# Reordering the first unit of a sparse-attention and feed-forward kernel: k, then v, then q, with the small work spread over three engines and filler matmuls in the waits

## Chip, cores, metric

The kernel runs on one core of one Trainium2 chip. The metric is the device time of one execution in microseconds (us). Before: 264.52 us, median of 4 runs (264.51 to 264.59). Every run of this study was recorded in the fast state, so all comparisons are of fast runs with fast runs.

Names used: PE is TensorE's matmul, PEld its weight load, DVE is VectorE, ACT is ScalarE, POOL is GpSimd, SP is SyncE, which issues most DMAs here.

## The reference, cut

```python
# q, k, v: 4 batches, 8 heads, 768 positions, 64 wide
block, window = 32, 16
k_sum = k.reshape(B, H, nb, block, D).max(axis=3)        # 24 block keys per head
v_sum = v.reshape(B, H, nb, block, D).mean(axis=3)
scores_l = scale * q @ k^T, masked to |i - j| < window
scores_s = scale * q @ k_sum^T + log(block)
a = softmax(concat(scores_l, scores_s));  out = a @ concat(v, v_sum)
# then, for the 3072 tokens of width 512:
h = x @ w_in (512 -> 2048);  g = h * sigmoid(1.702 h);  y = g @ w_out (2048 -> 512)
```

## The kernel before

The 3072 tokens are done in eight units (4 batches, two halves of 384 positions). A unit is attention for four pairs of heads, then `ff_in` (64 matmuls into `ph`, Gelu on ACT into `gT`) and `ff_out` (matmuls into `po`). The attention of unit u+1 is placed between the `ff_out` matmuls of unit u. Only the first unit's attention has nothing to hide behind, and it is the part that the change touches.

Local keys and block keys of 64 queries form one 128-row tile: own rows, halo rows, and 24 block rows. `kx` holds the keys in this form and `vw` the values. In the profile lines, `qz` is the transposed q, `ps_s` the scores, `a_sb` the masked exponentials, `ps_av` the values matmul, `x_sb` the attention output, and `xT` its transpose, which `ff_in` reads. The v windows are built by `vrows`: after the block sums of v (`vs`, a matmul with the selector `E`), four SBUF-to-SBUF DMAs copy the halo rows and two more copy the 24 block rows into every window.

```python
    def load_k(b, p):
        t = stage.tile([128, 2, 2, JH, D], F32, name=f"kf{p}", tag=f"kf{p}")
        for half in range(2):
            sp.dma_start(out=t[:, half].rearrange("p h r d -> p h (r d)"),
                         in_=k[b, 2 * p:2 * p + 2, half * HALF:(half + 1) * HALF]
                         .rearrange("h (p r) d -> p h (r d)", r=JH))
        raw["k", p] = t

    def load_q(b, p, half):
        t = stage.tile([128, 2, JH, D], F32, name=f"qf{p}{half}", tag=f"qf{p}{half}")
        sp.dma_start(out=t.rearrange("p h r d -> p h (r d)"),
                     in_=q[b, 2 * p:2 * p + 2, half * HALF:(half + 1) * HALF]
                     .rearrange("h (p r) d -> p h (r d)", r=JH))
        raw["q", p, half] = t

    def load_v(b):
        for c in range(3):
            t = stage.tile([128, H, 2, D], F32, name=f"vf{c}", tag=f"vf{c}")
            for j in range(2):
                r0 = (2 * c + j) * 128
                sp.dma_start(out=t[:, :, j, :],
                             in_=v[b, :, r0:r0 + 128].rearrange("h p d -> p h d"))
            raw["v", c] = t
# ...
    vs_ps = [None]

    def vsum(s, js):
        if js[0] == 0:
            vs_ps[0] = psx.tile([128, H * D], F32, name="ps_vs", tag="x")
        ps = vs_ps[0]
        w5 = vw[s].rearrange("p (j e) h c -> p j e h c", e=2)
        for j in js:
            o = 20 - 4 * j
            pe.matmul(out=ps, lhsT=E[:, o:o + 128], rhs=w5[:, j, 0, :, 0:D],
                      start=(j == 0), stop=(j == NJ - 1))

    def vrows(s):
        w5 = vw[s].rearrange("p (j e) h c -> p j e h c", e=2)
        dve.tensor_copy(out=vs[:, :, 0:D], in_=vs_ps[0].rearrange("p (h d) -> p h d", d=D))

        sp.dma_start(out=w5[96:112, 1:NJ, 0], in_=w5[112:128, 0:NJ - 1, 1])
        sp.dma_start(out=w5[112:128, :, 0], in_=w5[64:80, :, 1])
        sp.dma_start(out=w5[32:48, :, 1], in_=w5[48:64, :, 0])
        sp.dma_start(out=w5[48:64, 0:NJ - 1, 1], in_=w5[0:16, 1:NJ, 0])
        sp.dma_start(out=w5[64:64 + nb, :, 0], in_=vs[64:64 + nb].unsqueeze(1)
                     .to_broadcast([nb, NJ, H, VC]))
        sp.dma_start(out=w5[0:nb, :, 1], in_=vs[0:nb].unsqueeze(1)
                     .to_broadcast([nb, NJ, H, VC]))
# ...
    def tq(p, half, e0, e1):
        src = cast.pop(("q", p))
        big = psb.tile([128, 1024], F32, name="ps_q", tag="big")
        ps = big[:, 0:HALF]
        p3 = ps.rearrange("p (c r) -> p r c", r=JH)
        for r in range(JH):
            pe.matmul(out=p3[:, r], lhsT=src[:, r].rearrange("p h d -> p (h d)"),
                      rhs=ident, start=True, stop=True)
        for hh, eng in ((0, e0), (1, e1)):
            r = slice(hh * 64, hh * 64 + 64)
            copy(eng, qz[p][half][r, :, hh, :], ps[r].rearrange("p (t c) -> p t c", c=QT))
# ...
    def scores(b, half, p):
        a_sb[p] = attp.tile([128, 2, TH, QT], BF16, name="a_sb", tag="a_sb")
        a = a_sb[p]
        big = psb.tile([128, 1024], F32, name="ps_s", tag="big")
        ps = big[:, 0:2 * HALF].rearrange("p (t h c) -> p t h c", h=2, c=QT)
        for i in range(TH):
            pe.matmul(out=ps[:, i].rearrange("p h c -> p (h c)"),
                      lhsT=kx[p][b % 2][:, half * TH + i, :],
                      rhs=qz[p][half][:, i].rearrange("p h c -> p (h c)"),
                      start=True, stop=True)
        act.activation(out=a.rearrange("p h t c -> p t h c"), in_=ps,
                       func=ACT.Exp, scale=scale)
        af = a.rearrange("p h t c -> p h (t c)")
        dve.tensor_mul(af, af, mk[:, half * TH:(half + 1) * TH, :]
                       .rearrange("p t c -> p (t c)").unsqueeze(1)
                       .to_broadcast([128, 2, TH * QT]))

    def values(b, half, p):
        x_sb[p] = attp.tile([128, JH, 2, D], BF16, name="x_sb", tag="x_sb")
        a = a_sb[p]
        big = psb.tile([128, 1024], F32, name="ps_av", tag="big")
        ps = big.rearrange("p (h c) -> p h c", h=2)
        pv = ps[:, :, 0:390].rearrange("p h (j c) -> p h j c", c=130)
        for hh in range(2):
            for j in range(JH):
                t = half * TH + 2 * j
                pe.matmul(out=pv[:, hh, j, :].rearrange("p (e c) -> p e c", e=2),
                          lhsT=a[:, hh, 2 * j:2 * j + 2, :].rearrange("p t c -> p (t c)"),
                          rhs=vw[b % 2][:, t:t + 2, 2 * p + hh, 0:D + 1],
                          start=True, stop=True)

        rc = attp.tile([128, 2, JH, 2], F32, name="rc", tag="rc")
        dve.reciprocal(out=rc, in_=pv.rearrange("p h j (e c) -> p h j e c", e=2)[..., D])
        xo = x_sb[p].rearrange("p j h d -> p h j d")
        for e in range(2):
            r = slice(e * 64, e * 64 + 64)
            dve.tensor_mul(xo[r], pv[r, :, :, e * 65:e * 65 + D],
                           rc[r, :, :, e:e + 1].to_broadcast([64, 2, JH, D]))

    def tx(p):
        src = x_sb.pop(p)
        ps = psx.tile([128, HALF], BF16, name="ps_x", tag="x")
        for j in range(JH):
            pe.transpose(out=ps[:, j * 128:(j + 1) * 128],
                         in_=src[:, j].rearrange("p h d -> p (h d)"), identity=ident)
        dve.tensor_copy(out=xT[p], in_=ps)


    def ff_in(u, nt):
        ph = pmm.tile([128, HALF], F32, name="ph", tag="mm")
        for ko in range(KO):
            pe.matmul(out=ph, lhsT=w_in_sb[:, ko, nt * 128:(nt + 1) * 128],
                      rhs=xT[ko], start=(ko == 0), stop=(ko == KO - 1))
        act.activation(out=gT[u % 2][:, nt, :], in_=ph, func=ACT.Gelu_apprx_sigmoid)
```

The weights `w_in` and `w_out` are each loaded in four DMAs on POOL's queue, with a cast from float32 to bfloat16 on the way. The program of the first unit, in order (each engine runs its own part of it in this order):

```python
    load_k(0, 0)
    load_k(0, 1)
    load_v(0)
    load_k(0, 2)
    load_k(0, 3)
    load_q(0, 0, 0)
    load_q(0, 1, 0)

    for p in range(NP):
        clear_kx(dve, p, 0)
    clear_vw(dve, 0)
    dve.memset(vs[:, :, D:VC], float(block))
    cast_k(dve, 0)
    cast_k(act, 1)
    tk(0, 0)
    for p in range(NP):
        clear_qz(pool, p, 0)
    build_masks()
    tk(1, 0)
    for c in range(3):
        for j in (2 * c, 2 * c + 1):
            cast_v(act, 0, j, 0)
            cast_v(pool, 0, j, 1)
        vsum(0, (2 * c, 2 * c + 1))
    vrows(0)
    load_q(0, 2, 0)
    load_q(0, 3, 0)
    for p in range(NP):
        load_q(0, p, 1)
    cast_k(pool, 2)
    cast_k(act, 3)
    tk(2, 0)
    tk(3, 0)
    cast_q(pool, 0, 0)
    tq(0, 0, act, act)
    cast_q(pool, 1, 0)
    load_w_in(0)
    scores(0, 0, 0)
    tq(1, 0, act, act)
    cast_q(pool, 2, 0)
    scores(0, 0, 1)
    values(0, 0, 0)
    tq(2, 0, act, act)
    cast_q(pool, 3, 0)
    scores(0, 0, 2)
    values(0, 0, 1)
    tx(0)
    tq(3, 0, act, act)
    scores(0, 0, 3)
    values(0, 0, 2)
    tx(1)
    values(0, 0, 3)
    tx(2)
    tx(3)
    for c in range(1, 4):
        load_w_in(c)
    for c in range(4):
        load_w_out(c)
    for p in range(NP):
        clear_kx(pool, p, 1)
        clear_qz(pool, p, 1)
    clear_vw(pool, 1)
```

The softmax here doesn't subtract the row's maximum and nothing guards it: scores larger than these inputs give would overflow.

Of the kernel before, what the change touches and what calls it, by code (L numbers as in the profile page):

```python
# [34 lines left out]
def kernel(  # L35
# [75 lines left out]


    E = consts.tile([128, 20 + 128], BF16, name="E")
    nc.gpsimd.memset(E, 0.0)
    for c0 in (20, 84):
        sub = E[:, c0:c0 + 4]
        nc.gpsimd.memset(sub, 1.0)
        nc.gpsimd.affine_select(out=sub, in_=sub, compare_op=ALU.is_ge, fill=0.0,
                                base=0, pattern=[[-block, 4]], channel_multiplier=1)
        nc.gpsimd.affine_select(out=sub, in_=sub, compare_op=ALU.is_ge, fill=0.0,  # L120
                                base=block - 1, pattern=[[block, 4]],
                                channel_multiplier=-1)
# [4 lines left out]
    def sel(ap, base, cq, cp):  # L127
        nc.gpsimd.affine_select(out=ap, in_=ap, compare_op=ALU.is_ge, fill=0.0,
                                base=base, pattern=[[cq, QT]], channel_multiplier=cp)
# [1 line left out]
    mk = consts.tile([128, NQ, QT], BF16, name="mk")  # L131
    left = consts.tile([128, QT], BF16, name="left")

    def build_masks():
        for par, own, blk, halo in ((0, 0, 64, 96), (1, 64, 0, 32)):
            mid = 2 + par
            nc.gpsimd.memset(mk[:, mid, :], 1.0)
            sel(mk[own:own + 64, mid, :], window - 1, -1, 1)
            sel(mk[own:own + 64, mid, :], window - 1, 1, -1)
            sel(mk[blk:blk + 32, mid, :], nb - 1, 0, -1)  # L140
            hm = mk[halo:halo + 32, mid, :]

            sel(hm, -(QT - 16 - (window - 1)), 1, -1)
            sel(hm, -16, 0, 1)
            lf = left[halo:halo + 32, :]

            nc.gpsimd.memset(lf, 1.0)
            sel(lf, window - 1 - 16, -1, 1)
            sel(lf, 15, 0, -1)

            if par == 0:
                nc.gpsimd.tensor_copy(out=mk[:, 0, :], in_=mk[:, mid, :])
            else:
                nc.gpsimd.tensor_copy(out=mk[:, NQ - 1, :], in_=mk[:, mid, :])
                nc.gpsimd.tensor_copy(out=mk[halo:halo + 32, NQ - 1, :], in_=lf)
            nc.gpsimd.tensor_add(hm, hm, lf)
        nc.gpsimd.tensor_copy(out=mk[:, 1, :], in_=mk[:, 3, :])
        for t in range(4, NQ - 1):
            nc.gpsimd.tensor_copy(out=mk[:, t, :], in_=mk[:, 2 + t % 2, :])


    kx = [[keep.tile([128, NQ, 128], BF16, name=f"kx{p}_{s}") for s in range(2)]
# [17 lines left out]
    def clear_qz(eng, p, s):  # L180
        eng.memset(qz[p][s][0:64, :, 1, :], 0.0)
        eng.memset(qz[p][s][64:128, :, 0, :], 0.0)
# [18 lines left out]
    def copy(eng, out, in_):  # L201
        if eng is act:
            act.activation(out=out, in_=in_, func=ACT.Copy)
        else:
            eng.tensor_copy(out=out, in_=in_)

    def cast_k(eng, p):
        t = castp.tile([128, 2, JH, 2, D], BF16, name="kb", tag="kb")
        for half in range(2):
            copy(eng, t[:, half].rearrange("p r h d -> p h r d"), raw["k", p][:, half])  # L210
        cast["k", p] = t

    def cast_q(eng, p, half):
# [4 lines left out]
    def cast_v(eng, s, j, par):  # L218
        dst = vw[s].rearrange("p (j e) h c -> p j e h c", e=2)[:, j, par, :, 0:D]
        copy(eng, dst, raw["v", j // 2][:, :, j % 2, :])  # L220
# [3 lines left out]
    def vsum(s, js):  # L224
# [4 lines left out]
        for j in js:  # L229
            o = 20 - 4 * j  # L230
            pe.matmul(out=ps, lhsT=E[:, o:o + 128], rhs=w5[:, j, 0, :, 0:D],
                      start=(j == 0), stop=(j == NJ - 1))

    def vrows(s):
        w5 = vw[s].rearrange("p (j e) h c -> p j e h c", e=2)
        dve.tensor_copy(out=vs[:, :, 0:D], in_=vs_ps[0].rearrange("p (h d) -> p h d", d=D))
# [10 lines that stand above are left out]
    def at(ap, start, dims):  # L247
        a = ap[:, start:start + 1]
        return bass.AP(tensor=a.tensor, offset=a.offset, ap=[a.ap[0]] + dims)

    def tk(p, s, own=dve):
        src = cast.pop(("k", p))
        big = psb.tile([128, 1024], F32, name="ps_k", tag="big")
        for half in range(2):
            p3 = big[:, half * 512:half * 512 + HALF].rearrange("p (c r) -> p r c", r=JH)
            for r in range(JH):
                pe.matmul(out=p3[:, r], lhsT=src[:, half, r].rearrange("p h d -> p (h d)"),
                          rhs=ident, start=True, stop=True)

        flat = kx[p][s].rearrange("p t c -> p (t c)")  # L260
        copy(own, at(flat, 0, [[768, 2], [256, JH], [192, 2], [1, 64]]),
             at(big, 0, [[512, 2], [128, JH], [64, 2], [1, 64]]))
        ks = attp.tile([128, nb], BF16, name="ks", tag="ks")
        dve.tensor_reduce(out=ks.rearrange("p (h n) -> p h n", h=2),
                          in_=at(big, 0, [[512, 2], [block, nb // 2], [1, block]]),
                          axis=AX.X, op=ALU.max)

        dve.tensor_copy(out=at(flat, 256 + 96, [[768, 2], [256, 2], [-176, 2], [1, 16]]),
                        in_=at(big, 128 - 16, [[512, 2], [128, 2], [16, 2], [1, 16]]))
        dve.tensor_copy(out=at(flat, 768 + 96, [[-176, 2], [1, 16]]),  # L270
                        in_=at(big, HALF - 16, [[512 - HALF + 16, 2], [1, 16]]))
        dve.tensor_copy(out=at(flat, 128 + 32, [[768, 2], [256, JH], [-48, 2], [1, 16]]),
                        in_=at(big, 64 - 16, [[512, 2], [128, JH], [16, 2], [1, 16]]))
        dve.tensor_copy(out=at(flat, 64, [[256, NJ], [64, 2], [1, nb]]),
                        in_=ks.unsqueeze(1).unsqueeze(1).to_broadcast([128, NJ, 2, nb]))

    def tq(p, half, e0, e1):
        src = cast.pop(("q", p))
        big = psb.tile([128, 1024], F32, name="ps_q", tag="big")
        ps = big[:, 0:HALF]  # L280
        p3 = ps.rearrange("p (c r) -> p r c", r=JH)
        for r in range(JH):
# [5 lines that stand above are left out]
# [39 lines left out]
            dve.tensor_mul(xo[r], pv[r, :, :, e * 65:e * 65 + D],  # L327
                           rc[r, :, :, e:e + 1].to_broadcast([64, 2, JH, D]))

    def tx(p):  # L330
        src = x_sb.pop(p)
        ps = psx.tile([128, HALF], BF16, name="ps_x", tag="x")
        for j in range(JH):
            pe.transpose(out=ps[:, j * 128:(j + 1) * 128],
                         in_=src[:, j].rearrange("p h d -> p (h d)"), identity=ident)
        dve.tensor_copy(out=xT[p], in_=ps)


    def ff_in(u, nt):
# [19 lines left out]
            sp.dma_start(out=out[r0:r0 + 128, :], in_=osb)  # L359


    load_k(0, 0)
    load_k(0, 1)
    load_v(0)
    load_k(0, 2)
    load_k(0, 3)
    load_q(0, 0, 0)
    load_q(0, 1, 0)

    for p in range(NP):  # L370
        clear_kx(dve, p, 0)
    clear_vw(dve, 0)
    dve.memset(vs[:, :, D:VC], float(block))
    cast_k(dve, 0)
    cast_k(act, 1)
    tk(0, 0)
    for p in range(NP):
        clear_qz(pool, p, 0)
    build_masks()
    tk(1, 0)  # L380
    for c in range(3):
        for j in (2 * c, 2 * c + 1):
            cast_v(act, 0, j, 0)
            cast_v(pool, 0, j, 1)
        vsum(0, (2 * c, 2 * c + 1))
    vrows(0)
    load_q(0, 2, 0)
    load_q(0, 3, 0)
    for p in range(NP):
        load_q(0, p, 1)  # L390
    cast_k(pool, 2)
    cast_k(act, 3)
    tk(2, 0)
    tk(3, 0)
    cast_q(pool, 0, 0)
    tq(0, 0, act, act)
    cast_q(pool, 1, 0)
    load_w_in(0)
    scores(0, 0, 0)
    tq(1, 0, act, act)  # L400
    cast_q(pool, 2, 0)
    scores(0, 0, 1)
    values(0, 0, 0)
    tq(2, 0, act, act)
    cast_q(pool, 3, 0)
    scores(0, 0, 2)
    values(0, 0, 1)
    tx(0)
    tq(3, 0, act, act)
    scores(0, 0, 3)  # L410
    values(0, 0, 2)
    tx(1)
    values(0, 0, 3)
    tx(2)
    tx(3)
    for c in range(1, 4):
        load_w_in(c)
    for c in range(4):
# [108 lines left out]
```

## Time and profile before

| | before |
|---|---|
| median | 264.52 us |
| span in the trace | 263.1 us |
| first values matmul (`ps_av`) | 27.3 us |
| first `ff_in` matmul (`ph`) | 39.6 us |
| first `ff_out` matmul (`po`) | 53.8 us |
| second unit's first `ph` | 67.7 us |

How to read it: the span counts from the first instruction; times of events are from there. In a chain of waits, each line is start, duration, and what took it, followed back from the end. A duration of 0.16 us per `ph` matmul (384 columns) is PE at full clock (called warm below), 0.32 is half clock (cold). The lines themselves are in the prediction.

### The profile page before, as it was taken

How to read it: one execution, taken by the hardware profiler on the slowest of the kernel's cores; microseconds unless marked ns; L12 is line 12 of the kernel's file. 1: busy time of each engine (PE TensorE's matmuls, PEld its weight loads, DVE VectorE, ACT ScalarE, POOL GpSimd, SP SyncE). 2: the span in 40 equal slices, each digit the busy share in tenths (PEclk: the TensorE clock that was granted, in tenths of full speed). 3: DMA queues.
4: the chain of work that ended last, by engine and by line, in shares of the span. 5: the costliest groups of instructions: out<-in, count | busy, mean ns of one | idle time of the engine just before them, and what ended most of it. 6: DMA issues, size and time to landing. Idle time of an engine off the chain costs nothing.

```text
span 263.1 us, 4275 instructions
## 1 busy us (share of the span) xinstructions
PE 234.2 (89%) x1571; PEld 142.0 (54%) x1592; DVE 146.7 (56%) x336; ACT 131.3 (50%) x218; POOL 75.5 (29%) x185
## 2 busy tenths in 40 slices
PE   2543749999998999999989999999989999999994
PEld 1131535656665555655665656566656556555541
DVE  4527471447699483358796754276995745372000
ACT  3524443663644627752646446844446366637711
POOL 8890792735203003840202006820220000000000
PEclk9998555999999999999999999999999999999999
DMA  6969999998432118993150129972130210011012
GB/s 176 227 173 178 306 202 196 196 221 259 171 52 55 40 42 223 229 272 117 42 103 0 42 92 249 261 239 83 22 81 2 81 40 2 9 71 42 0 40 81
DMA packets 52981, 32.34 MB, mean 123 GB/s; under 512 B 26848, under 2 KB 49888, under 8 KB 52960
## 3 DMA queue, kind: packets, MB, share of 16 engines
q1 hardware_dynamic: 48736, 27.88, 41.9%
q0 software_dynamic: 4224, 4.19, 9.7%
q8 instruction: 12, 0.20, 0.3%
q14 instruction: 9, 0.07, 0.1%
HBM read 27.26 MB, written 6.29 MB: 128 GB/s over the span
## 4 chain that ended last, share of the span: by engine, by line
PE 74%; DVE 8%; POOL 6%; ACT 5%; DMA 2%; issue 2%; SPq 1%; ACTq 0%; POOLq 0%
PE po L27 29%; PE ph L27 26%; PE ps_s L27 4%; PE ps_q L27 4%; PE ps_av L27 4%; DVE kx L27 4%; PE ps_x L27 3%; DMA qf<-in_q_dram 2%; PE ps_k L27 2%; DVE ks L27 2%; ACT L27 2%; DVE x_sb L27 2%; PE ps_vs L27 1%; POOL qz L27 1%; POOL vw L27 1%
## 5 line engine op out<-in xcount | busy, mean ns | idle before, releaser
L27 PE MATMUL ph<-xT,w_in_sb 128*128 128x384 bf16 x512 | 97.7, 335 | 0.7 <-ACT gT L27 0.7
L27 PE MATMUL po<-w_out_sb,gT 128*128 128x512 bf16 x363 | 92.5, 379 | 0.8
L27 ACT ACTIVATE gT<-ph 128x384 bf16<-128x384 f32 x128 | 61.6, 490 | 46.3 <-PE ph L27 45.7
L27 PEld LDWEIGHTS <-w_in_sb 128*128 128x128 bf16 x512 | 52.6, 106 | 31.2 <-issue 5.2
L27 PEld LDWEIGHTS <-gT 128*128 128x128 bf16 x384 | 34.6, 97 | 28.0
L27 DVE CAST qz<-ps_q 64x384 bf16<-64x384 f32 x56 | 31.1, 555 | 28.6 <-PE ps_q L27 28.0
L27 POOL CAST qb<-qf 128x384 bf16<-128x384 f32 x32 | 16.1, 513 | 101.5 <-PE ps_q L27 63.6
L27 DVE TENSOR_TENSOR a_sb<-a_sb,mk 128x768 bf16<-128x768 bf16 x32 | 18.4, 575 | 33.8 <-ACT a_sb L27 32.9
L27 ACT ACTIVATE a_sb<-ps_s 128x768 bf16<-128x768 f32 x32 | 25.2, 809 | 23.4 <-PE ps_s L27 23.3
L27 DVE TENSOR_TENSOR x_sb<-ps_av,rc 64x384 bf16<-64x384 f32 x64 | 35.5, 555 | 1.5
L27 ACT ACTIVATE osb<-po 128x512 f32<-128x512 f32 x24 | 14.3, 597 | 41.1 <-PE ps_x L27 23.3
L27 DVE CAST kx<-ps_k 128x768 bf16<-128x768 f32 (+1 forms) x64 | 25.5, 439 | 10.3 <-PE ps_k L27 10.3
L27 POOL CAST vw<-vf 128x512 bf16<-128x512 f32 x42 | 24.6, 620 | 7.5 <-DMA vf<-in_v_dram 7.3
L27 PE MATMUL ps_k<-ident,kb 128*128 128x128 bf16 x96 | 15.5, 351 | 7.6 <-DVE kb L27 3.9
L27 POOL CAST kb<-kf 128x384 bf16<-128x384 f32 x26 | 13.5, 542 | 29.2 <-PE ps_k L27 26.5
L27 ACT ACT_TABLE_LOAD x16 | 20.5, 1283 | 1.1 <-PEq L511 0.8
L27 PE MATMUL ps_q<-ident,qb 128*128 128x128 bf16 x96 | 16.7, 316 | 4.6 <-DVE kx L27 3.4
L27 PE MATMUL ps_s<-qz,kx 128*128 128x128 bf16 x192 | 16.8, 227 | 4.3 <-ACT qz L27 4.3
L27 PEld LDWEIGHTS <-kx 128*128 128x128 bf16 x192 | 13.9, 102 | 10.4 <-issue 4.1
L27 PEld LDWEIGHTS <-a_sb 128*128 128x128 bf16 x192 | 14.4, 102 | 7.7 <-DVE a_sb L27 0.8
L27 PE MATMUL ps_av<-vw,a_sb 128*128 128x130 bf16 x192 | 17.6, 231 | 0.6 <-DVE a_sb L27 0.5
L27 PEld LDWEIGHTS <-kb 128*128 128x128 bf16 x96 | 11.2, 139 | 11.8 <-POOL kb L27 4.4
(42 smaller groups left out, 115.0 us busy)
## 6 DMA issues: line engine op xcount, KB each, us to landing
kf<-in_k_dram SPq DMA_DIRECT2D x32, 192.0 KB, 4.0
vf<-in_v_dram SPq DMA_DIRECT2D x24, 256.0 KB, 5.1
qf<-in_q_dram SPq DMA_DIRECT2D x32, 192.0 KB, 4.2
out_dram<-osb SPq DMA_DIRECT2D x24, 256.0 KB, 2.0
w_in_sb<-in_moe_w_in_dram POOLq DMA_DIRECT2D x4, 512.0 KB, 10.0
w_out_sb<-in_moe_w_out_dram POOLq DMA_DIRECT2D x4, 512.0 KB, 20.5
vw<-vs SPq DMA_DIRECT2D x8, 148.5 KB
vw<-vw SPq DMA_DIRECT2D x8, 99.0 KB, 2.9
```

The lines of the kernel that those rows point to most:

```text
L27: r = f(*a, **kw)
```

## The change

Its intent: let all k work run while v loads, let q arrive before it is needed, take work off POOL (masks, clears) so that nothing waits for it, split casts and copies over ACT, DVE and POOL, and keep PE's clock up with matmuls on a zero tile whose result nobody reads. The diff, cut to its core:

```diff
     E = consts.tile([128, 20 + 128], BF16, name="E")
-    nc.gpsimd.memset(E, 0.0)
+    warm = consts.tile([128, 512], BF16, name="warm")
+    dve.memset(warm, 0.0)
+    dve.memset(E, 0.0)
     for c0 in (20, 84):
         sub = E[:, c0:c0 + 4]
-        nc.gpsimd.memset(sub, 1.0)
+        dve.memset(sub, 1.0)
# ... the mask code: the 14 selections stay on GpSimd (now all before anything else), and
#     the memsets, copies and adds of build_masks() become finish_masks() on VectorE:
+    def finish_masks():
+
+        dve.tensor_copy(out=mk[:, 0, :], in_=mk[:, 2, :])
+        dve.tensor_copy(out=mk[:, NQ - 1, :], in_=mk[:, 3, :])
+        dve.tensor_copy(out=mk[32:64, NQ - 1, :], in_=left[32:64, :])
+        for par, halo in ((0, 96), (1, 32)):
+            hm = mk[halo:halo + 32, 2 + par, :]
+            dve.tensor_add(hm, hm, left[halo:halo + 32, :])
+        dve.tensor_copy(out=mk[:, 1, :], in_=mk[:, 3, :])
+        dve.tensor_copy(out=mk[:, 4:6], in_=mk[:, 2:4])
+        dve.tensor_copy(out=mk[:, 6:10], in_=mk[:, 2:6])
+        dve.tensor_copy(out=mk[:, 10, :], in_=mk[:, 2, :])
# ...
-    def cast_k(eng, p):
+    def cast_k(eng, p, eng2=None):
         t = castp.tile([128, 2, JH, 2, D], BF16, name="kb", tag="kb")
         for half in range(2):
-            copy(eng, t[:, half].rearrange("p r h d -> p h r d"), raw["k", p][:, half])
+            copy((eng2 or eng) if half else eng, t[:, half].rearrange("p r h d -> p h r d"), raw["k", p][:, half])
# ...
+    def warmth(n):
+
+        for i in range(n):
+            ps = pmm.tile([128, 512], F32, name="ps_w", tag="mm")
+            pe.matmul(out=ps, lhsT=warm[:, 0:128], rhs=warm, start=True, stop=True)
# ... tk() is split in two: tk_own (transposes and own columns, copy on ACT) and tk_rest (maxima, halos)
-    def tq(p, half, e0, e1):
+    def tq(p, half, e0, e1, early=False):
         src = cast.pop(("q", p))
-        big = psb.tile([128, 1024], F32, name="ps_q", tag="big")
+        big = (pmm.tile([128, 512], F32, name="ps_q1", tag="mm") if early else
+               psb.tile([128, 1024], F32, name="ps_q", tag="big"))
# ...
-    def tx(p):
+    def tx(p, eng=dve):
         src = x_sb.pop(p)
         ps = psx.tile([128, HALF], BF16, name="ps_x", tag="x")
         for j in range(JH):
             pe.transpose(out=ps[:, j * 128:(j + 1) * 128],
                          in_=src[:, j].rearrange("p h d -> p (h d)"), identity=ident)
-        dve.tensor_copy(out=xT[p], in_=ps)
+        copy(eng, xT[p], ps)
# ...
-    load_k(0, 0)
-    load_k(0, 1)
+    for p in range(NP):
+        load_k(0, p)
     load_v(0)
-    load_k(0, 2)
-    load_k(0, 3)
-    load_q(0, 0, 0)
-    load_q(0, 1, 0)
-
+    for p in range(NP):
+        load_q(0, p, 0)
     for p in range(NP):
         clear_kx(dve, p, 0)
     clear_vw(dve, 0)
     dve.memset(vs[:, :, D:VC], float(block))
-    cast_k(dve, 0)
-    cast_k(act, 1)
-    tk(0, 0)
     for p in range(NP):
-        clear_qz(pool, p, 0)
-    build_masks()
-    tk(1, 0)
-    for c in range(3):
-        for j in (2 * c, 2 * c + 1):
-            cast_v(act, 0, j, 0)
-            cast_v(pool, 0, j, 1)
-        vsum(0, (2 * c, 2 * c + 1))
+        clear_qz(dve, p, 0)
+    warmth(8)
+
+    cast_k(act, 0, dve)
+    big0 = tk_own(0, 0, act)
+    cast_k(act, 1, dve)
+    tk_rest(0, 0, big0)
+    big1 = tk_own(1, 0, act)
+    cast_k(pool, 2)
+    tk_rest(1, 0, big1)
+    cast_k(pool, 3)
+    warmth(2)
+    cast_v(act, 0, 0, 1)
+    cast_v(pool, 0, 0, 0)
+    big2 = tk_own(2, 0, act)
+    vsum(0, (0,))
+    cast_v(act, 0, 1, 1)
+    cast_v(pool, 0, 1, 0)
+    tk_rest(2, 0, big2)
+    vsum(0, (1,))
+    big3 = tk_own(3, 0, act)
+    for j in (2, 3, 4, 5):
+        cast_v(act, 0, j, 1)
+        cast_v(pool, 0, j, 0)
+        if j == 2:
+            tk_rest(3, 0, big3)
+            finish_masks()
+        warmth(1)
+        vsum(0, (j,))
+    cast_q(dve, 0, 0)
+    cast_q(pool, 1, 0)
     vrows(0)
-    load_q(0, 2, 0)
-    load_q(0, 3, 0)
     for p in range(NP):
         load_q(0, p, 1)
-    cast_k(pool, 2)
-    cast_k(act, 3)
-    tk(2, 0)
-    tk(3, 0)
-    cast_q(pool, 0, 0)
-    tq(0, 0, act, act)
-    cast_q(pool, 1, 0)
+    tq(0, 0, act, dve, True)
+    cast_q(dve, 2, 0)
+    tq(1, 0, act, dve, True)
+    cast_q(pool, 3, 0)
     load_w_in(0)
     scores(0, 0, 0)
-    tq(1, 0, act, act)
-    cast_q(pool, 2, 0)
+    tq(2, 0, act, dve, True)
     scores(0, 0, 1)
+    tq(3, 0, act, dve, True)
+    scores(0, 0, 2)
+    warmth(1)
     values(0, 0, 0)
-    tq(2, 0, act, act)
-    cast_q(pool, 3, 0)
-    scores(0, 0, 2)
+    scores(0, 0, 3)
+    warmth(1)
     values(0, 0, 1)
-    tx(0)
-    tq(3, 0, act, act)
-    scores(0, 0, 3)
+    warmth(2)
+    tx(0, act)
     values(0, 0, 2)
-    tx(1)
+    warmth(2)
+    tx(1, act)
     values(0, 0, 3)
-    tx(2)
-    tx(3)
+    warmth(3)
+    tx(2, act)
+    warmth(3)
+    tx(3, act)
     for c in range(1, 4):
         load_w_in(c)
     for c in range(4):
```

The weights are still the next thing on POOL's queue after the last q cast. In the kernel before, that queue stopped at the cast of a late q (27.6 us), and so the seven later weight loads went out from 28.9. In the changed kernel all eight go out from 19.3 on. The issue of `w_in` (shortest, median and longest in ns, then first and last start in us), before:

```profile
L27 POOL DMA_DIRECT2D w_in_sb<-in_moe_w_in_dram x4: 746/756/908, 18.8 to 30.4; - x4
```

and in the changed kernel:

```profile
L27 POOL DMA_DIRECT2D w_in_sb<-in_moe_w_in_dram x4: 750/766/881, 19.3 to 21.7; - x4
```

More of the change, by code (lines that the diff above doesn't have):

```diff
@@ L132 @@
     left = consts.tile([128, QT], BF16, name="left")
-    def build_masks():
-        for par, own, blk, halo in ((0, 0, 64, 96), (1, 64, 0, 32)):
-            mid = 2 + par
-            nc.gpsimd.memset(mk[:, mid, :], 1.0)
-            sel(mk[own:own + 64, mid, :], window - 1, -1, 1)
-            sel(mk[own:own + 64, mid, :], window - 1, 1, -1)
-            sel(mk[blk:blk + 32, mid, :], nb - 1, 0, -1)
-            hm = mk[halo:halo + 32, mid, :]
-            sel(hm, -(QT - 16 - (window - 1)), 1, -1)
-            sel(hm, -16, 0, 1)
-            lf = left[halo:halo + 32, :]
-            nc.gpsimd.memset(lf, 1.0)
-            sel(lf, window - 1 - 16, -1, 1)
-            sel(lf, 15, 0, -1)
-            if par == 0:
-                nc.gpsimd.tensor_copy(out=mk[:, 0, :], in_=mk[:, mid, :])
-            else:
-                nc.gpsimd.tensor_copy(out=mk[:, NQ - 1, :], in_=mk[:, mid, :])
-                nc.gpsimd.tensor_copy(out=mk[halo:halo + 32, NQ - 1, :], in_=lf)
-            nc.gpsimd.tensor_add(hm, hm, lf)
-        nc.gpsimd.tensor_copy(out=mk[:, 1, :], in_=mk[:, 3, :])
-        for t in range(4, NQ - 1):
-            nc.gpsimd.tensor_copy(out=mk[:, t, :], in_=mk[:, 2 + t % 2, :])
@@ new lines @@
+    dve.memset(mk, 1.0)
+    dve.memset(left, 1.0)
+    for par, own, blk, halo in ((0, 0, 64, 96), (1, 64, 0, 32)):
+        mid = 2 + par
+        sel(mk[own:own + 64, mid, :], window - 1, -1, 1)
+        sel(mk[own:own + 64, mid, :], window - 1, 1, -1)
+        sel(mk[blk:blk + 32, mid, :], nb - 1, 0, -1)
+        sel(mk[halo:halo + 32, mid, :], -(QT - 16 - (window - 1)), 1, -1)
+        sel(mk[halo:halo + 32, mid, :], -16, 0, 1)
+        sel(left[halo:halo + 32, :], window - 1 - 16, -1, 1)
+        sel(left[halo:halo + 32, :], 15, 0, -1)
@@ L251, in tk, with tk_own @@
     def tk(p, s, own=dve):
+        tk_rest(p, s, tk_own(p, s, own))
+    def tk_own(p, s, own):
         src = cast.pop(("k", p))
@@ L262, in tk, with tk_rest @@
              at(big, 0, [[512, 2], [128, JH], [64, 2], [1, 64]]))
+        return big
+    def tk_rest(p, s, big):
+        flat = kx[p][s].rearrange("p t c -> p (t c)")
         ks = attp.tile([128, nb], BF16, name="ks", tag="ks")
```

## The prediction

> **What bounds the kernel now.** I read the page's slices first, then the engine-busy table by stage, the chain of waits over the first 70 us, the SyncE queue's timeline, and last the groups of single tiles.
>
> The slices (40 of 6.6 us each):
>
> ```profile
> PE   2543749999998999999989999999989999999994
> PEclk9998555999999999999999999999999999999999
> DMA  6969999998432118993150129972130210011012
> ```
>
> TensorE (PE) is 90% busy or more nearly everywhere after slice 6. Only the first six slices have room, and they coincide with the half-speed clock (slices 4 to 6). So the change, which touches only the first unit, can gain only there. The same by stage (columns: stretch, its length, busy us of PE, PEld, DVE, ACT, POOL, then granted clock, DMA share, GB/s):
>
> ```profile
> 0.00:20.00 20.00, 8.90 (x30) 4.33 (x30) 8.16 (x35) 7.11 (x11) 17.51 (x63) 1.00 0.89 191
> 20.00:39.60 19.60, 10.33 (x75) 7.57 (x74) 12.38 (x30) 8.40 (x13) 11.31 (x36) 0.61 1.13 230
> 39.60:53.80 14.20, 14.20 (x78) 8.43 (x77) 4.80 (x9) 7.28 (x15) 6.50 (x13) 0.82 1.22 196
> 53.80:67.70 13.90, 13.79 (x108) 8.06 (x108) 8.90 (x19) 6.26 (x10) 5.68 (x9) 1.00 0.96 254
> ```
>
> The first feed-forward matmul starts at 39.6 us; from there PE never idles. In the first 20 us POOL is 88% busy. From 39.6 to 53.8 PE is full, but part of it at clock 0.82. The DMA engines stay at a share of 1.13 to 1.22 until 54 us.
>
> The chain over 20 to 47 us (start, us, what):
>
> ```profile
> 20.28 0.80 SPq L27
> 21.12 6.46 DMA qf<-in_q_dram
> 27.64 0.51 POOL qb L27
> 28.19 0.83 PE ps_q L27 x3
> ...
> 38.31 0.56 DVE x_sb L27
> ...
> 39.79 5.10 PE ph L27 x16
> 45.22 1.95 PE ph L27 x12
> ```
>
> What holds the start is one load: the q of heads 4 and 5 is issued at 21.1, because it stands on the SyncE queue behind the v-window copies, and lands at 27.6. From its cast to the first ph takes another 12 us of serial small steps. Then 16 ph take 5.10 us (0.319 each), where later 12 take 1.95 (0.163): half speed until 44.9. The SyncE queue:
>
> ```profile
> 0.82 1.98 SPq L27 DMA_DIRECT2D kf<-in_k_dram  x4
> 2.83 6.66 SPq L27 DMA_DIRECT2D vf<-in_v_dram  x6
> 9.54 2.68 SPq L27 DMA_DIRECT2D kf<-in_k_dram  x4
> 12.26 0.98 SPq L27 DMA_DIRECT2D qf<-in_q_dram  x2
> 16.49 2.73 SPq L27 DMA_DIRECT2D vw<-vw  x4
> 19.32 1.75 SPq L27 DMA_DIRECT2D vw<-vs  x2
> 21.12 3.83 SPq L27 DMA_DIRECT2D qf<-in_q_dram  x6
> ```
>
> **What the Trainium skill says.** "TensorE: Matmul & The Clock Gate", Part 1, says the array idles at half clock and reaches full clock after about 3.4 us of sustained work, and drops back after a similar idle window. The trace agrees: full rate returns 5 us after ph starts. It also shows that the printed clock of 1.00 in the first 20 us is no evidence, because the first v sums there run at the slow duration (maximum) and all later ones at 379 ns:
>
> ```profile
> L27 PE MATMUL ps_vs<-vw,E x24: 379/379/586, 8.2 to 187.7; 128*128 128x512 bf16 x24
> ```
>
> "DMA: Bandwidth & Descriptors", Queues, rings and completion order, says each engine takes turns between queues packet by packet. The trace fits: beside the weights the six v loads of the next batch (256-byte rows) take 23.69 us to issue, against 6.66 us alone. "SBUF — State Buffer", Who interferes with whom, says VectorE with two SBUF inputs and a GpSimd that reads SBUF exclude each other. The trace hints at it: two masks beside GpSimd casts at 56.75 took 1.47 us, where two alone would take 1.12. "ScalarE: Activation LUTs", What ACT_TABLE_LOAD costs, gives 1283 ns, and the trace has 1283 for each.
>
> **The change part by part.**
>
> (1) Load order. All twelve k and q loads of the first half and six v loads go out before anything waits. Rates from the trace: a 256 KB v load lands each 1.2 us (v casts on ACT begin at 7.53, 8.71, 9.93, 11.13, 12.34, 13.42); after the last v, four k loads of 192 KB were there by 15.85, so 0.6 us each. The v loads therefore move from 13.4 to about 13.4 + 4 x 0.6 = 15.8 us, and the four q loads end at 15.8 + 4 x 0.6 = 18.2 us instead of 27.6 for the third. Removed from the path: 9.4 us of waiting for q.
>
> (2) Masks, clears, casts. POOL loses 8 qz clears (16 in the window are 6.9 us, so 3.5) and some 14 mask copies, memsets and adds of 0.15 to 0.3 (about 3). With 14 mask selections of 0.25, 4 of E at 0.19 and gaps it is done near 6.6 us, when k of heads 4 and 5 arrives. VectorE's added clears (about 3 us, estimated from its 0.22 us for the 128x192 clear) delay k of heads 0 and 1 by perhaps 1 us. All k work then lies beside the v loads: k takes about 1.8 us of VectorE per pair (0.95 maximum, 0.64 halos, 0.22 copy) and one 0.8 us copy on ACT; four pairs end near 14.3, masks near 15.7. Both are before q arrives. Cost on the path: 0.
>
> (3) Values cannot start before the v windows are complete. The last v is cast at 16.45; the copies on SyncE begin about then, as now (16.49), and end issuing at 21.1, as now. With 2.7 us to land (measured for the vw copies) they are there at 23.8; I take 24.3, as the weights now run beside them. Meanwhile q is cast on VectorE and POOL, and ACT and VectorE share the eight qz copies (0.48 and 0.555). From 16.4, VectorE has 0.69 + 4 x 0.555 + 2 x 0.4 + 3 x 0.56 = 5.4 us, so three heads are masked near 22.9, before 24.3.
>
> (4) From 24.3: first values matmuls 0.5, then VectorE for four pairs: 0.23 + 2 x 0.555 = 1.34, with gaps 1.45 each, plus one mask of 0.56: 6.4 us. That is 31.2; last transpose 0.2 and the first ph can follow, near 31.4 instead of 39.6. Gain 8.2 us.
>
> (5) Fillers. Fourteen 512-column matmuls lie in stage 4; warm they take 14 x 0.22 = 3.1 us (estimate from 1.95/12 = 0.163 for 384 columns), cold 6.1. With 24 values, 6 score and 12 transpose matmuls, PE is loaded through most of the 7 us, so the clock should rise before or soon after ph starts. Fully warm, ph's 64 matmuls save 16 x (0.319 - 0.163) = 2.5 us. I take half, 1.3, because cold fillers can themselves delay the last transposes by 1 to 2 us.
>
> (6) Transposed copies move to ACT. The Gelu table load can then come only after the last of them, about 31.9 to 33.2. Three ph buffers cover 3 x 0.65 us, so at most 0.3 us is lost; I take 0.2.
>
> Later units have the same program, so their 56.8 us per batch stays. Sum: -8.2 - 1.3 + 0.2 = -9.3 us; 264.5 - 9.3 = **255.2 us**.
>
> **The rivals.**
>
> Rival A: the weights become the wait. They are issued on POOL; now the first at 18.77 and the rest from 28.9, and w_out lands late:
>
> ```profile
> DMA to landing us min/median/max: 16.6/20.5/24.5
> ```
>
> Issued at 31.1 to 33.3, these landings are about 47.7 to 57.8, 3.3 us apart. Parts of ff_out need them from 53.8 to 64.3, so 6 us of slack. After the change all eight are issued from 18.8 to about 25. At 3.3 us each, plus some 4 us lost to q and k of the next batch, the last lands at 18.8 + 2 + 8 x 3.3 + 4 = 51 to 52, and PE wants it at 31.4 + 12 + 10.3 = 53.7. For it speaks the DMA share, which is at its ceiling already; against it that the issue moves nearly as far as PE does. If it holds, 2 to 4 us come back: 257 to 259.
>
> Rival B: the v windows land later than 24.3, since their small packets share with twice the weights: each us is a us on the end; 256 to 258 with 26 us.
>
> Rival C: the filler matmuls pay fully and the windows land early, at 23: 264.5 - 9.5 - 2.5 = 252.5.
>
> Rival D: VectorE, with more work, slows POOL and itself (the shared port), adding 1 us to each of stages 2 and 4: 257. The chain in stage 4 is VectorE's already, so this is a small shift of the same bound.
>
> Rival E: the next batch's loads miss their date in unit 1. Its k casts are done by 62 and first used at 69 to 75; a shift by 9 leaves nearly nothing for pairs 2 and 3, but v also moves up once the weights are in. A loss of 1 to 2 us at worst.
>
> **Range and chances.** All the gain lies in when ph starts (31.4, give or take 2), whether the clock is up (0 to 2.5), and weights (0 to 3 lost). Taken together 252.0 to 258.6 should hold it 8 times in 10. The 2% line is at 259.2, a gain of 5.3; missing it takes two of A, B and D together: 0.08 for the same. Slower would need PE to be held by something not seen: 0.01.
>
> **What would show it.** Step 1: the q casts start at 16 to 18 us and none waits for a load at 27. Step 2: POOL's k casts near 6.6, VectorE idle before q. Step 3: the first ps_av at 24.3, ended by a DMA, not VectorE. Step 4: first ph at 31.4, the chain before it VectorE's x_sb. Step 5: ph at 0.163 from the start, or slow for part of the first 16. Step 6: a table load after the last xT. If ps_av waits to 26 or later, B is right; if ph or po idle on DMA with PE gaps between 31 and 55 us, A; if from 57 us on the two traces differ by other than a constant, E. A first ph near 31 with an end above 259 would prove my picture of the later stages wrong.

## The result and the profile after

The changed kernel takes 260.27 us (260.08 to 260.60, 4 runs) against 264.52. The ratio is 0.984 with a 95% interval of 0.982 to 0.986. A ratio here is the mean time of one kernel's fast runs over the mean of the other's of the same rounds, so it isn't quite the ratio of the medians. The gain is 4.25 us. The prediction had 9.3 us, that is 255.2, and a range that ended at 258.6; the measured time lies above it.

The slices of the changed kernel's page:

```profile
PE   7555499999989999999989999999989999999994
PEclk9986589999999999999999999999999999999999
DMA  6999999999350139982140249961321110111012
```

PE is now full after slice 5 (before: after slice 6), and the half-clock stretch is shorter. The DMA engines are 90% busy or more in slices 2 to 10. By stage (columns as in the prediction: stretch, its length, busy us of PE, PEld, DVE, ACT, POOL, clock, DMA share, GB/s):

```profile
0.00:20.00 20.00, 12.34 (x51) 6.10 (x52) 14.89 (x67) 9.75 (x15) 12.23 (x37) 0.92 0.95 207
20.00:37.00 17.00, 10.62 (x77) 7.74 (x78) 9.65 (x20) 5.45 (x9) 11.45 (x36) 0.69 1.14 207
37.00:49.30 12.30, 12.03 (x79) 7.61 (x78) 4.44 (x8) 8.84 (x17) 2.49 (x5) 1.00 1.20 216
49.30:63.20 13.90, 13.79 (x108) 8.03 (x108) 9.22 (x19) 6.26 (x10) 9.21 (x15) 1.00 1.05 252
```

The stage before the first `ph` ends at 37.0 instead of 39.6 (2.6 us), `ff_in` takes 12.3 us instead of 14.2 (1.9 us), and `ff_out` takes 13.9 as before. That is 4.5 us, and the spans of the two traces differ by 4.4 at the end: the later units keep their time. POOL fell from 17.5 to 12.2 us in the first 20 us, DVE rose from 8.2 to 14.9.

The chain of waits of the changed kernel, 20 to 40 us:

```profile
20.76 8.12 DMA vw<-vs
...
29.01 0.82 PE ps_av L27 x6
...
36.87 0.35 PE ps_x L27 x3
...
37.25 0.49 ACT xT L27
...
37.75 1.28 ACT L27
...
39.05 0.50 ACT gT L27
...
39.59 0.81 PE ph L27 x4
```

The q load is gone from the chain. In its place stands the copy of the block rows into the v windows, 8.12 us for 148.5 KB. Values can't start before it lands, so the first values matmul is *later* than before, 29.0 instead of 27.3. All that stands between values and `ph` is faster: 8.0 us instead of 12.3. Behind the last transposed copy stands the Gelu table load (the nameless ACT entry of 1.28 us). The first 12 `ph` run before its end, at full rate:

```profile
37.05 2.36 PE L27 MATMUL ph<-xT,w_in_sb 128*128 128x384 bf16 x12
```

### The profile page after: what moved, and what is told of

Same layout as the page of the kernel before. It is cut to its first block, busy times and chain, and to the rows that moved or that the text cites. A ratio compares the mean times of both kernels' runs of the same rounds, so it can differ in the third digit from the quotient of the medians.

```text
span 258.7 us, 4314 instructions
## 1 busy us (share of the span) xinstructions
PE 235.8 (91%) x1596; PEld 143.2 (55%) x1618; DVE 151.1 (58%) x357; ACT 132.7 (51%) x220; POOL 69.9 (27%) x157
## 4 chain that ended last, share of the span: by engine, by line
PE 75%; DVE 10%; DMA 5%; ACT 5%; SPq 2%; issue 1%; POOL 0%; ACTq 0%; DVEq 0%
PE po L27 29%; PE ph L27 25%; PE ps_av L27 5%; DVE kx L27 4%; PE ps_q L27 4%; PE ps_s L27 4%; PE ps_x L27 3%; DMA vw<-vs 3%; PE ps_k L27 3%; ACT L27 2%; DVE ks L27 2%; DMA vf<-in_v_dram 2%; SPq L27 2%; DVE x_sb L27 2%; PE ps_vs L27 2%
## 5 line engine op out<-in xcount | busy, mean ns | idle before, releaser
L27 PE MATMUL ph<-xT,w_in_sb 128*128 128x384 bf16 x512 | 95.5, 329 | 0.9 <-ACT gT L27 0.8
L27 ACT ACTIVATE gT<-ph 128x384 bf16<-128x384 f32 x128 | 61.4, 491 | 39.5 <-PE ph L27 38.7
L27 PEld LDWEIGHTS <-w_in_sb 128*128 128x128 bf16 x512 | 51.8, 104 | 30.4 <-issue 3.6
L27 DVE CAST qz<-ps_q 64x384 bf16<-64x384 f32 x60 | 33.3, 555 | 28.4 <-PE ps_q L27 26.8
L27 POOL CAST qb<-qf 128x384 bf16<-128x384 f32 x30 | 15.2, 512 | 97.4 <-PE ps_q L27 69.2
L27 ACT ACTIVATE a_sb<-ps_s 128x768 bf16<-128x768 f32 x32 | 25.2, 810 | 27.5 <-PE ps_s L27 27.3
L27 DVE TENSOR_TENSOR x_sb<-ps_av,rc 64x384 bf16<-64x384 f32 x64 | 35.5, 555 | 1.5
L27 DVE TENSOR_TENSOR a_sb<-a_sb,mk 128x768 bf16<-128x768 bf16 x32 | 19.1, 599 | 28.2 <-ACT a_sb L27 27.2
L27 POOL CAST vw<-vf 128x512 bf16<-128x512 f32 x42 | 25.2, 639 | 12.3 <-DMA vf<-in_v_dram 12.2
L27 DVE CAST kx<-ps_k 128x128 bf16<-128x128 f32 (+3 forms) x60 | 21.7, 405 | 5.7 <-PE ps_k L27 5.7
L27 POOL CAST kb<-kf 128x384 bf16<-128x384 f32 x28 | 14.7, 544 | 29.8 <-PE ps_k L27 24.4
L27 PEld LDWEIGHTS <-a_sb 128*128 128x128 bf16 x192 | 14.1, 101 | 13.1 <-issue 5.5
L27 ACT ACT_TABLE_LOAD x16 | 20.5, 1283 | 1.1 <-PEq L542 0.8
L27 PEld LDWEIGHTS <-kx 128*128 128x128 bf16 x192 | 14.5, 106 | 6.2 <-issue 1.2
L27 DVE TENSOR_REDUCE ks<-ps_k 128x24 bf16<-128x768 f32 x16 | 15.2, 949 | 1.7 <-ACT kx L27 1.6
L27 PEld LDWEIGHTS <-qb 128*128 128x128 bf16 x96 | 9.8, 120 | 10.0 <-issue 3.2
## 6 DMA issues: line engine op xcount, KB each, us to landing
w_in_sb<-in_moe_w_in_dram POOLq DMA_DIRECT2D x4, 512.0 KB, 12.2
vw<-vs SPq DMA_DIRECT2D x8, 148.5 KB
```

Source lines behind the costliest of these rows:

```text
L27: r = f(*a, **kw)
```

## The experiments

**Theory 1.** The block-row copies are starved by the weight loads, which the change lets go out beside them. **Rival 1:** the copies take 8 us by their own shape (24 partitions, broadcast source). **Rival 2:** the q and k loads that follow them on the SP queue slow them. Each experiment below starts from the changed kernel unless it says otherwise; before stands for the kernel before, run on the same chip in the same call (264.6 to 265.1 us).

### e1: the weights only after the block rows

```diff
+    pool.tensor_copy(out=seen[64:64 + nb], in_=w5[64:64 + nb, NJ - 1, 0, 0, 0:8])   # waits for the
+    pool.tensor_copy(out=seen[0:nb], in_=w5[0:nb, NJ - 1, 1, 0, 0:8])               # two row copies
     load_w_in(0)
```

> The change, with all eight weight loads held back until both block-mean row copies have landed (a tiny read of their last rows on GpSimd ahead of the first weight load). Theory 1 (the block-mean rows are starved because the weights run beside them): the first values matmul moves from 29.0 to 23.5 to 25 us, the first ph from 37.0 to 31.5 to 33.5; the weights then start about 5 us later, so the last w_out lands near 57 to 58 where it is wanted near 54, and 2 to 4 us come back as PE gaps: 257 to 259.5 in all. Rival 1 (the copy takes 8 us by its own shape, broadcast and small rows on 24 partitions): the first values matmul stays at 28.5 to 29.5 and the total is 260 to 266. Rival 2 (the q and k loads issued behind it on the same queue slow it): the same 28 to 29.5 as rival 1.

Measured: 259.69 us (258.00 to 260.12), ratio 0.980 (0.976 to 0.984); its median is just past the expected band. Of its chain of waits:

```profile
21.00 3.24 DMA vw<-vs
...
24.91 9.18 DMA w_in_sb<-in_moe_w_in_dram
```

And of its PE timeline:

```profile
31.23 0.34 PE L27 MATMUL ps_x<-ident,x_sb 128*128 128x128 bf16 x3 [0.43 <-DVE x_sb L27]
34.14 2.10 PE L27 MATMUL ph<-xT,w_in_sb 128*128 128x384 bf16 x6 [2.57 <-DMA w_in_sb<-in_moe_w_in_dram]
```

The same copy took 3.24 us instead of 8.12. Both rivals fall: the shape is unchanged, and the q and k loads still follow on the queue. Values started at 24.4 (predicted 24.3), and PE had the last transposes behind it at 31.57 (predicted: `ph` at 31.4). So with the rows on time, the prediction's steps 3 and 4 hold as written. But now the first weights came at 34.1 and PE waited 2.57 us for them, and after that idle it ran cold: the first 16 `ph` took 5.30 us. What was gained on the rows was paid to the weights, though not where the expectation had it: the last `w_out` landed near 58 as expected, but no matmul waited for it.

### e5: one weight load ahead, seven held back

The two small reads of e1 stand behind `load_w_in(0)` here, in front of the other seven loads.

> The change, with the first weight load where it is and the other seven held until the block-mean rows have landed. Theory 1 with the weights served in order: the rows land about when the first weight load is through, 25 to 27.5 (24.2 with none ahead, 28.9 with all eight); ph from 33.5 to 35.5 without waiting for its first weights; the last weights land near 55 to 58, close to where they are wanted: total 257 to 259.5. If seven loads behind the first make no difference to the rows (only the first one beside them counts), they land at 28.5 to 29 and the total is 260 or more.

Measured: 259.21 us (258.56 to 259.64), ratio 0.978 (0.975 to 0.980). Its chain has:

```profile
20.75 6.97 DMA vw<-vs
```

The rows landed at 27.7. So none ahead: 24.2; one ahead: 27.7; all eight: 28.0 in one run, 28.9 in another (29.4 in e3). One 512 KB load beside the rows does most of the harm. GpSimd had issued it by 20.3, before the copy's wait of 6.97 us began, which points to the load in flight and not to its issuing. The kernel before has just such a single load ahead of its rows, too, but its values begin at 27.3 for other reasons (b1). An estimate: a second row copy issued there at 20.3 and taking the same 7 us lands at 27.3, just in time; no trace shows when it landed. The rows landed just past the expected 25 to 27.5, `ph` started at 35.5, and the total was in the expected band; 0.978 against the change's 0.982 to 0.984 isn't a separation that the intervals carry with certainty.

### e2: the block rows written on chip

```diff
+            act.activation(out=w5[0:nb, 0:JH, 1], in_=vs[0:nb].unsqueeze(1)
+                           .to_broadcast([nb, JH, H, VC]), func=ACT.Copy)
+            pool.tensor_copy(out=w5[64:64 + nb, 0:JH, 0], in_=vs[64:64 + nb].unsqueeze(1)
+                             .to_broadcast([nb, JH, H, VC]))
-        sp.dma_start(out=w5[64:64 + nb, :, 0], ...)     # all six windows
+        sp.dma_start(out=w5[64:64 + nb, JH:NJ, 0], ...) # windows 3 to 5 only; the same for 0:nb
```

> The change, with the block-mean rows of the three windows that the first unit needs written by ACT (rows 0 to 23) and GpSimd (rows 64 to 87), about 1.5 to 2.7 us each; only windows 3 to 5 still come by DMA. If the landing of these rows is what held the values (theory 1 and rival 1 alike): first values matmul at 23 to 25 us, ph at 31 to 33, total 254 to 257, and the weights, now wanted some 6 us earlier and issued some 2 us later, may cost 1 to 2 us of it. If the weights also starve the four window copies that go out just before them, the values start at 25 to 27 instead and the total is 256 to 259. If something else held the values, no gain: 260.

Measured: 256.09 us (256.00 to 256.43), ratio 0.968 (0.966 to 0.970), inside the expected band. Of its chain:

```profile
18.76 1.52 ACT vw L27
20.28 0.38 ACT qz L27
```

Values started at 25.0, `ph` at 32.9. The 1.52 us row copy on ACT stands ahead of the first q copy, so some of the wait went from the DMA to ACT. Still, 260.3 became 256.1: most of the 5.1 us that the prediction missed hung on these rows.

### e3: the transposed copies on VectorE

```diff
-    tx(0, act)        # the same for 1, 2, 3
+    tx(0)
```

> The change, with the four transposed copies of the first unit back on VectorE. Theory: the Gelu table load (37.75 to 39.05) then comes before the last copy instead of behind it, ph no longer waits for gT at 39.6, worth 0.5 to 0.8 us: 259.5 to 259.8. Rival: VectorE is the chain in this stage, four copies of 0.36 us are on it, and three of them delay the last x_sb by 0.7 to 1.1: net 260 to 260.8, or no change.

Measured: 260.62 us (259.69 to 261.12), ratio 0.984 (0.982 to 0.987): no change, as the rival said. Of its chain:

```profile
37.60 0.37 DVE xT L27
...
38.34 2.72 PE ph L27 x16
```

`ph` runs through without the table wait, but starts later: at 38.2, after values at 29.5. That is 8.7 us for the stage against 8.0, since DVE carries the copies between its other work.

### e4 and f1: no fillers; f0: the change again

```diff
-        for i in range(n):
+        for i in range(0):        # in warmth()
```

> The change without any filler matmul. If the fillers warm the clock: the last values and the first 10 to 16 ph run at 0.32 instead of 0.163 us, 1.5 to 2.5 us lost, less 0.3 to 0.8 gained since no cold filler stands ahead of a transpose: 261.2 to 262.4. Rival: the values and score matmuls alone would have warmed it, or ph warms itself beside the table load, so the fillers do nothing: 259.8 to 260.5.

e4 measured: 260.36 us, but spread from 258.93 to 261.69, ratio 0.984 (0.979 to 0.988): inconclusive. So it was run once more, with the change itself beside it in the same rounds:

> The change itself, unedited, on the same chip and in the same rounds as the run without fillers: 260.0 to 260.6, and the same wait of about 5 us for the block-mean rows.

> The change without any filler, once more, as the first run of it was not clear. From its first trace (first 16 ph 4.76 instead of 2.6 us, but the table load hidden behind them and the last transpose 0.4 earlier): 0.8 to 1.5 us more than the change of the same rounds, so 261.0 to 261.8. If fillers are worth nothing in all: within 0.4 of it.

f0: 260.30 us (259.12 to 260.59), ratio 0.982 (0.980 to 0.985). f1: 261.57 us (260.94 to 261.76), ratio 0.987 (0.985 to 0.990). Of f1's chain:

```profile
37.03 4.77 PE ph L27 x16
```

The 16 `ph` take 4.77 us, near the half clock, where the change has them at full rate save for the table wait. The fillers are worth 1.3 us in the medians of f0 and f1; the two intervals just touch, and e4 alone showed no difference. The traces agree with each other: from the first `ph` to the first `po` it is 13.9 us without fillers (e4, f1) and 12.3 with them (the change, f0), of which 0.2 goes back because the fillers let `ph` start 0.2 us later (37.0 against 36.8, with equal rows).

### b1: the kernel before, only the q loads early

```diff
     load_q(0, 1, 0)
+    load_q(0, 2, 0)
+    load_q(0, 3, 0)
 # ...
     vrows(0)
-    load_q(0, 2, 0)
-    load_q(0, 3, 0)
```

> The kernel before, with one edit: the q loads of pairs 2 and 3 go out right behind those of pairs 0 and 1, ahead of the window copies. The reading of the prediction (that one late q load holds the start) would give q casts near 19 instead of 27.6 and a first ph several us earlier than 39.6: 256 to 262 in all. Theory 1 says otherwise: GpSimd, no longer stopped by the late q, issues the seven other weight loads from about 20 instead of 28.9, the block-mean rows land beside them at 28 to 29.5, the first values matmul moves from 27.3 to 28 to 30 and the end stays or gets later: 264 to 267.

Measured: 264.61 us (264.36 to 264.74), ratio 0.998 (0.996 to 1.000) against before. Of its chain:

```profile
27.24 0.81 PE ps_av L27 x6
...
28.09 0.81 PE ps_q L27 x3
...
39.68 5.12 PE ph L27 x16
```

The late q load of pair 2 was the longest entry of the chain before, 6.46 us, and taking it away moved `ph` from 39.79 to 39.68. PE gets to this pair's q at 28.1 in any case, because k of pairs 2 and 3, then scores and values pair by pair, stand ahead of it in program order. The chain was right that the load ended last at that point, but a second path ended 0.1 us earlier. Theory 1's own number for the rows (28 to 29.5) was not met either: values started at 27.2 without waiting for a DMA. With one weight load ahead of them (the other seven went out only from 22.7) the rows must have landed by 27.2; in e5 they did at 27.7.

### b2: b1 with the block rows on chip

The edit is that of b1 with that of e2.

> The kernel before, with the early q loads and with the block-mean rows of the first three windows on chip too. The run with early q alone changed nothing, and its first values matmul at 27.2 waited for no DMA. If the order of the small steps (k of pairs 2 and 3 after v, q casts and scores one pair at a time between the values) holds the first unit there, also this one changes little: 263.5 to 264.8. If the rows were a hidden second wait at 27 behind the q, the values start at 24 to 25 and the total is 261 to 262.5.

Measured: 266.24 us (265.74 to 267.25), ratio 1.006 (1.004 to 1.008): slower, outside the expected band. Of its chain:

```profile
17.14 1.51 POOL vw L27
...
18.71 0.51 POOL kb L27
...
19.27 1.48 PE ps_k L27 x6
```

POOL's row copy stands ahead of its k cast, which came at 17.0 before and at 18.7 here, and everything after moved by 1.7 to 2.3 us: values from 27.2 to 29.3, `ph` from 39.5 to 41.8. So the test of whether the rows were a hidden second wait failed, because the edit delayed something else. What it shows instead is what held the first unit before: the k cast of pair 2 on POOL (pair 3's is on ACT), and the serial steps behind it. That is what the change's order takes away.

### d1, d2, d3: towards the best version

All have the rows on chip. d1 puts only the last transposed copy back on DVE (`tx(3)`). d2 also moves the mask copies and adds to POOL, in the gaps between its v casts, save the last two, which stay on DVE behind the first values. d3 is d2 with both row copies on POOL, after the last q cast, and none on ACT.

> The change with the block-mean rows of windows 0 to 2 written on chip, and only the last of the four transposed copies on VectorE, so that the Gelu table load can go before it. Theory: ph starts near 32.8 as with the rows alone and its wait for the table (35.4) goes: 0.5 to 0.9 us less than the rows alone, so 255.2 to 255.6. If the copies' engine does not matter: 256.1.

> As the run with the rows on chip and the last transposed copy on VectorE, and the mask copies moved from VectorE to GpSimd, between its v casts, where it idles 0.6 us of each 1.2. The prediction's step 2 said they cost nothing on the path; the chain shows them ahead of the first q cast (17.6 where q is there at 16.5). If the chain is right, the first q cast starts 0.8 to 1.2 us earlier and ph with it: 254.0 to 254.8. If step 2 is right: no difference to the run without it, within 0.3.

> Rows on chip, last transposed copy on VectorE, masks on GpSimd as before, but both row copies on GpSimd after the last q cast, so that ACT is free for the qz copies. Values start near 23 and ph near 30.7 instead of 32.6. The weights are issued 1.4 us later, from 21.5, and the last lands near 54.5, where PE would want it at 52.7. If the weights now bind: 254.3 to 255.3, with PE gaps that end on a DMA in the first ff_out. If they keep up: 253.2 to 253.8. If VectorE binds whatever ACT does: 255.2.

| | median (range), us | ratio to before (95%) | first `ps_av` | first `ph` |
|---|---|---|---|---|
| d1 | 255.64 (255.40 to 256.38) | 0.965 (0.963 to 0.967) | 24.6 | 32.5 |
| d2 | 255.26 (255.22 to 255.69) | 0.963 (0.961 to 0.966) | 24.3 | 32.4 |
| d3 | 255.71 (255.08 to 257.81) | 0.967 (0.964 to 0.970) | 22.0 | 30.1 |

d1 is 0.3% below e2 in ratio, 0.5 us in the medians: about the table wait, but the intervals overlap. In d2, DVE's first q cast began at 16.42 (d1: 17.39), but no gain can be told apart from the noise; the next step in its chain is ACT's row copy again. d3 started `ph` 2.3 us earlier than d2 and ended no earlier. Its chain and its waits (total us, times, longest) say why:

```profile
24.88 19.04 DMA w_out_sb<-in_moe_w_out_dram
...
43.97 1.04 PE po L27 x4
```

```profile
PE ph L27 <- DMA w_in_sb<-in_moe_w_in_dram: 0.8, 1, 0.8
```

Now PE waits for weights: 0.79 us for the last part of `w_in` and 0.26 us for the first of `w_out`, through which the chain runs. These and a q cast (0.33 us) are 1.4 of the 2.1 us by which `ff_in` is longer than in d2 (13.9 against 11.8); the rest is not accounted for. The expectation had the weights binding, but in `ff_out` only, and at 254.3 to 255.3 us. That is rival A of the prediction, and here it binds only once the steps ahead of it are out of the way. d2 has the lowest median, 3.7% under the kernel before and about 5 us under the change; its lead over d1 and d3 is within the noise.

## Why the prediction was wrong

- **Step 1, load order: right.** The q casts began at 17.0, 17.6, 18.9 and 19.9 us (16 to 18 was said); that at 17.0 came as its q landed, and the later ones waited for DVE or PE and not for a load. But the value put on it, 9.4 us "removed from the path", wasn't there to remove: b1 shows that the wait for q before had a second path 0.1 us behind it. This did not enter the sum, which went from the new path's own times.
- **Step 2, masks, clears and casts at no cost: right in effect.** POOL's first k cast came at 6.9 (predicted 6.6). The masks on DVE ended at 17.6, not 15.7, and delayed the first q cast by about 1 us, but the rows hid it; d2 found no certain gain from moving them. Rival D's slower VectorE shows there in single operations (the two mask adds took 0.84 us, in d1 0.38), and it does not in the stage of step 4 (two `x_sb` products take 1.12 us before and after).
- **Step 3 is the step that failed.** The row copies were issued nearly when it said (the issue ends at 21.6; predicted 21.1), but "I take 24.3, as the weights now run beside them" put 0.5 us on an effect that measured 4.6: they landed at 28.9 (28.0 to 29.4 in other traces with the same loads), and at 24.2 with the weights held back (e1). Its 2.7 us to land were also those of other copies, the halo rows; a row copy took 3.24 us even in e1. The mechanism was named, as rival B with "each us is a us on the end", but it was sized at 26 at most. The range was too narrow on just that side, and this one rival was enough to miss the 2% line, for which the prediction had thought two were needed.
- **Step 4: right.** In e1 values began at 24.4 and PE was free for `ph` at 31.57, against 24.3 and 31.4. In the changed kernel, with a cold PE at the start of the stage after 5.4 us without work, it took 8.0 us instead of 7.1: 0.9 us of the miss.
- **Step 5, fillers: the mechanism was right, and the size by two errors that cancel.** PE runs at full rate from 34 us on, before `ph` starts. So the first 16 `ph` gained all that a full clock gives, 2.2 us against f1 and 2.5 against the kernel before, where the prediction took half, 1.3. The larger loss of step 6 and the later start took it back to about 1.4 in the traces, 1.3 in the medians; that this equals step 5's number is luck.
- **Step 6, table load: the place was right, the size too low.** It stands behind the last xT, at 37.75, and PE loses some 0.6 us (12.3 us for `ff_in` where 11.7 would be full rate throughout), not 0.2, as 12 `ph` fit into the three buffers and the thirteenth waits for gT.
- **Rival A** did not bind in the change: the last `w_out` landed at 24.6 + 28.7 = 53.3 and was wanted near 60. PE waited for weights in e1 and d3, each time for a part of `w_in` first. **Rival E** is not seen: the distance of the two traces is 4.5 us at 49.3 us and 4.4 at the end. **Rival C** asked for windows at 23 us; they came at 28.9.
- **Two readings.** The printed clock is at 5 in slices 5 to 7, not 4 to 6, so the half speed reaches into a slice in which PE is already full; step 5 counted that part. And the prediction says that the trace agrees with 3.4 us of work before full clock; its own lines show 5.1 us (39.79 to 44.89).

The sum: `ph` at 37.0 instead of 31.4 is 5.6 us, of which 4.7 is the rows and 0.9 the stage behind them; `ff_in` at 12.3 us instead of the 13.1 that steps 5 and 6 imply (14.2 - 1.3 + 0.2) gives 0.8 back. That makes 4.8 of the 5.1 us between 255.2 and 260.3.

What stays open: why exactly the rows lose so much. Rows of 1056 bytes taking turns with the weights' packets is a reading that fits, but no run varied the packet size, and it stays unshown.

## What to carry to other kernels

When a change lets a bulk load go out earlier, list the small transfers that are in flight at that moment and have someone waiting for them: here 8 us for 148.5 KB instead of 3.2. A small copy that the DMA engines would do beside bulk traffic was better done here by compute engines (e2). Such an engine needs 1.5 us to spare and nothing on the path behind the copy in its queue (b2 shows the price if something is). And the longest entry in a chain of waits is an upper bound of what its removal brings, not an estimate: look for who would have come second.

## What the Trainium skill lacked or had wrong

- "DMA: Bandwidth & Descriptors", Queues, rings and completion order, tells that an engine takes turns between queues packet by packet, but not what that costs a small transfer that someone waits for. The runs: a 148.5 KB copy issued from SyncE took 3.24 us with no GpSimd load ahead of it, 6.97 with one 512 KB load and 7.31 to 8.70 with eight. One load does most of the harm; a line with such numbers, and the warning that issuing bulk loads earlier can move a small copy onto the path, would have helped with step 3.
- "ScalarE: Activation LUTs", What ACT_TABLE_LOAD costs, gives 1283 ns for the load, and the trace agrees (1.28), plus a drain of about 1.38 us for each switch. No such drain is seen here: from the end of the last copy at 37.74 to the start of the Gelu at 39.05 there are 1.31 us in all.
- "TensorE: Matmul & The Clock Gate", Part 1, warns that clock events in a trace can't be trusted wholly, and the runs agree: among the eleven runs of the kernel before that stood beside f0, nine were recorded at a mean clock of 0.998 to 1.000 and two at 0.961, at times within 0.6% of each other. It gives the cold and warm times from one matmul to the next; what it lacks is the plain advice to take the recorded duration of a known matmul as the witness (in the kernel before, `ps_vs` took 0.58 us in the first 20 us and 0.379 later, with a printed clock of 1.00 both times).
